# Selections on TensorE for two chunks instead of four, direct placement for three instead of six, softplus written over its exponent in a ring of four tiles

## The chip, the cores and the metric

The kernel runs on one core of a Trainium2 chip. TensorE (PE in the profile, with its weight loads as PEld), VectorE (DVE), ScalarE (ACT), GpSimd (POOL) and the DMA queue that SyncE (SP) issues each work through their own list of instructions in order and meet through semaphores. The metric is the device time of one execution in microseconds; less is better.

## The reference, cut to what matters

Three parts follow one another. The first is a gated linear attention over 4 batches, 8 heads, 768 steps and head size 48: a complex state of 48x48 per head is multiplied at each step by a normed complex gate, the outer product of k and v is added, and q reads the state's real part. The second and third are feed-forward layers over the 3072 tokens of 384 features that come out:

```python
for t in range(S):
    new_re = ar * S_re - ai * S_im
    new_im = ar * S_im + ai * S_re
    S_re, S_im = (new_re + kv, new_im)
    y[:, :, t] = np.einsum('bhd,bhde->bhe', q[:, :, t], S_re)
# x = y as (3072, 384)
h = x @ w_in                                             # 384 -> 2048
g = np.maximum(h, 0.0) + np.log1p(np.exp(-np.abs(h)))    # softplus
x2 = g @ w_out                                           # 2048 -> 384
out = (((x2 @ w1) * (x2 @ w2)) @ w3) @ wo                # 384 -> 1024 -> 384
```

All data are float32 (the weights come as float64 words and are converted on the chip).

## The kernel before, in words

**Stages.** First the product of the last two weights is formed (`early`, tiles wpa, wpe). Phase A then runs over nine blocks of tokens (128, 256, then seven of 384): for each of 16 slices f of the 2048 inner features, `s1` forms h into a PSUM tile s1, ScalarE and VectorE turn it into softplus, and `s2a` adds its product with w_out into three accumulators acc. The first two blocks multiply in plain float32 (native); from block 2 on each operand is split into a high part (xh, gh, ww..h) and a low part (xl, gl, ww..l), and three products replace one. The attention for 24 chunks of 128 tokens (chunk u: 6 chunks per batch) is woven in between and must deliver x for a block before that block can start: chunk 0 for block 0, chunks 1 and 2 for block 1, chunks 3, 4 and 5 for block 2, and so on. Phase B runs the third layer over six blocks of 512 tokens.

**One chunk of attention.** VectorE norms the gates (`norm`, tiles nt, P) and multiplies them up in a scan over pairs of chunks (`scan`, tiles tm, P, E), then forms the scaled q (i = 0) and k (i = 1), real and imaginary, in the tile qkp, of which there is one (`inv`, steps s3 to s5, L641 to L655). Features stand on partitions there in groups of 128, so that heads of 48 straddle them. The tile rs (two of them, taken in turn) wants each head on its own, real part on partitions 0 to 47 and imaginary on 64 to 111. There are two ways: `pick(i)` (L657) selects with small matrices of ones on TensorE into PSUM tiles pk, and ScalarE copies them to rs; `s6` (L673) writes qkp to memory (pd) and reads it back as two transfers into rs. Chunks below `PICK` (L62) go the first way. In `mm(u)` TensorE transposes k (ktp to kT), forms the scores sc, which VectorE masks into am, and `heads` (L714) forms the outputs yp and the state step stp in one group. Chunks below `PLACE` (L63) have the columns of heads 6 and 7 put in their final rows by extra matmuls with the sparse operands ext, and x is read straight from PSUM; later chunks form plain heads, ScalarE copies them to the tile y (one of them) in two pieces, and six small transfers (L762 to L767) move the last two heads into place before x is read.

**Softplus** (L966 to L978). ScalarE writes Abs, Exp and Ln of h into a tile e (a ring of two), VectorE adds max(h, 0) and writes a tile g (a ring of three); from block 2 on ScalarE casts g to gh and VectorE forms gl = g - gh. In blocks 0 and 1 `s2a` reads g itself. The copies of the accumulators at a block's end (xoa) use the ring e as well.

**What sets the order.** Every call is only recorded (`Plan.add`) with a cost of its own and the instructions it must follow. `Plan.flush` orders all of them by a list schedule over 16 rounds of priorities and keeps the order that ends first by its own costs; the instructions are then issued in that order on each engine. Instructions inside `with plan.together()` (L230) form one entry that starts from a base cost. Any edit of what is recorded can therefore move instructions anywhere in the program. All instructions carry the line L207, where the recorded call is made; the tiles tell them apart.

Of the kernel before, what the change touches and what calls it, by code (L numbers as in the profile page):

```python
# [11 lines left out]
F32 = mybir.dt.float32  # L12
# [24 lines left out]
BLOCKS = [(0, 128), (128, 256)] + [(NB * i, NB) for i in range(1, NT // NB)]  # L37
NATIVE = 2
QKB = 1
GB = 3  # L40
HB = 5
AMB = 2
ATT = 5
# [15 lines left out]
CVS = 10  # L59
LEAD = 0  # L60
RATE = 340
PICK = 4  # L62
PLACE = 6  # L63
VW = 6 * 64 + 2 * D
ROUNDS = 16
SEED = 214
# [16 lines left out]
class Plan:  # L83
# [145 lines left out]
    @contextmanager  # L229
    def together(self):  # L230

        self.group = self.push(None, [], set(), 150, 0)
        yield
        self.group = None

# [127 lines left out]
def fused(ctx: ExitStack, tc: tile.TileContext, a_in, qk_in, v_in, wio, w12, w3t, wo2, q, k, v, a_re, a_im, outT):  # L363
# [262 lines left out]
    def inv(u):  # L626
        s = c[u]

        def s1():
            s["n2"] = ap.tile([P, 2, GT], F32, tag="n2", name=f"n2{u}")  # L630
            A.activation(out=s["n2"].rearrange("p c (a l) -> p c a l", l=LN), in_=half(u), func=AF.Square)

        def s2():
            n = s["n2"]
            V.tensor_tensor(out=n[:, 0], in0=n[:, 0], in1=n[:, 1], op=ALU.add)
            if u % CPB == CPB - 1:
                A.copy(pend[:, u // CPB], n[:, 0, GT - LN + J8 - 1 :: J8])
            A.activation(out=n[:, 1], in_=n[:, 0], func=AF.Ln, bias=eps_p)
            A.activation(out=n[:, 1], in_=n[:, 1], func=AF.Exp, scale=-1.0)

        def s3():  # L641
            s["qkp"] = ap.tile([P, 2, G, 2, T], F32, tag="qkp", bufs=QKB, name=f"qkp{u}")
            qkp(u, 0, s["qk"][:, 0])

        def s4():
            n = s["n2"]
            V.tensor_tensor(
                out=in_order(n[:, 0].rearrange("p (g t) -> p g t", t=T)),
                in0=by_group(gt(n[:, 1])),
                in1=in_order(s["qk"][:, 1].rearrange("p (g t) -> p g t", t=T)),  # L650
                op=ALU.mult,
            )

        def s5():
            qkp(u, 1, s["n2"][:, 0])  # L655

        def pick(i):  # L657
            s["rs"] = rs[u % 2]
            for hh in range(2):
                pt = att_ps([P, 4, T], f"pk{u}_{i}_{hh}")  # L660
                with plan.together():
                    for n in range(4):
                        h = 4 * hh + n
                        gs = [g for g in range(G) if (h, g) in sels]
                        for ri in range(2):
                            for g in gs:
                                PE.matmul(
                                    pt[64 * ri : 64 * ri + 64, n], sels[h, g], s["qkp"][:, ri, g, i],
                                    start=g == gs[0], stop=g == gs[-1],
                                )  # L670
                A.copy(s["rs"][:, 4 * hh : 4 * hh + 4, i], pt[0 : 64 + D])

        def s6():  # L673
            s["rs"] = rs[u % 2]
            SP.dma_start(
                pd[u].rearrange("(m p) n -> p m n", p=P), s["qkp"].rearrange("p c g q t -> p (c g) (q t)")
            )
            for ri in range(2):
                SP.dma_start(
                    s["rs"][ri * 64 : ri * 64 + D].rearrange("d h q t -> d h (q t)"),  # L680
                    pd[u][ri * DM : (ri + 1) * DM].rearrange("(h d) n -> d h n", d=D),
                )

        if u < PICK:
            return [s1, s2, s3, lambda: pick(0), s4, s5, lambda: pick(1)]
        return [s1, s2, s3, s4, s5, s6]
# [204 lines left out]
    def early():  # L891
        wo = []
        pieces = []
        for k in range(0, FB, 2):
            r = wp.tile([P, 2 * DM, 2], I32, tag=f"wb{k // 2}", name=f"wor{k}")
            for i in range(2):
                shifted(r[:, i * DM : (i + 1) * DM], wo2[k + i])
            wo.append(r)
        for m0 in range(0, FB, 3):
            n = min(3, FB - m0) * P  # L900
            for k in range(0, FB, 2):
                r = wp.tile([P, 2 * DM, 2], I32, tag=f"wb{4 + len(pieces) % 4}", name=f"w3r{m0}_{k}")[:, 0 : 2 * n]
                for i in range(2):
                    shifted(r[:, i * n : (i + 1) * n], w3t[k + i, :, 2 * m0 * P : 2 * (m0 * P + n)])
                j = len(pieces)
                if m0 == 0:
                    t = wp.tile([P, 2 * DM], F32, tag=f"wa{8 + k // 2}", name=f"wo{k}")
                    convert(t, wo[k // 2], next(ntop) % 2)
                    wo[k // 2] = t
                w = wp.tile([P, 2 * DM], F32, tag=f"wa{12 + j % 3}", name=f"w3_{m0}_{k}")[:, 0 : 2 * n]  # L910
                convert(w, r, next(ntop) % 2)
                pieces.append(w)
                if k == 0:
                    o = [
                        pst(f"acc{i}", 1, [P, NX], f"wpa{m0 + i}") if m0 != 3 else pst("s1", S1B, [P, NX], f"wpa{m0 + i}")
                        for i in range(n // P)
                    ]
                for h in range(2):
                    for i in range(n // P):
                        PE.matmul(  # L920
                            o[i][:, 0:DM], w[:, h * n + i * P : h * n + (i + 1) * P], wo[k // 2][:, h * DM : (h + 1) * DM],
                            start=(k + h == 0), stop=(k + h == FB - 1),
                        )
            for i in range(n // P):
                m = m0 + i
                e = sp.tile([P, NB], F32, tag="e", name=f"wpe{m}")
                A.copy(e, o[i][:, 0:DM])
                SP.dma_start(wpd[m // 2][:, (m % 2) * DM : (m % 2 + 1) * DM], e)

# [16 lines left out]
    def s1(bi, f):  # L946
        _, n = BLOCKS[bi]
        native = bi < NATIVE
        if bi == NATIVE:
            w_split(f)  # L950
        xh, xl = xt[bi]
        pt = pst("s1", S1B, [P, NB], f"s1_{bi}_{f}")
        o = pt[:, 0:n]
        if native:
            prods = [(w32[f], xh)]
        else:
            prods = [(ww[f][0], xh), (ww[f][1], xh), (ww[f][0], xl)]
        i = 0
        for w, xx in prods:
            for k in range(KC):  # L960
                PE.matmul(
                    o, w[:, k * P : (k + 1) * P], xx[:, k, 0:n],
                    start=(i == 0), stop=(i == len(prods) * KC - 1),
                )
                i += 1
        e = sp.tile([P, NB], F32, tag="e", name=f"e_{bi}_{f}")[:, 0:n]  # L966
        A.activation(out=e, in_=o, func=AF.Abs)
        A.activation(out=e, in_=e, func=AF.Exp, scale=-1.0)
        A.activation(out=e, in_=e, func=AF.Ln, bias=1.0)
        g = sp.tile([P, NB], F32, tag="g", bufs=GB, name=f"g_{bi}_{f}")[:, 0:n]  # L970
        V.scalar_tensor_tensor(out=g, in0=o, scalar=0.0, in1=e, op0=ALU.max, op1=ALU.add)
        if native:
            return g, None
        gh = sp.tile([P, NB], F32R, tag="gh", bufs=HB, name=f"gh_{bi}_{f}")[:, 0:n]
        gl = sp.tile([P, NB], F32R, tag="gl", bufs=HB, name=f"gl_{bi}_{f}")[:, 0:n]
        A.copy(gh, g)
        V.tensor_tensor(out=gl, in0=g, in1=gh.bitcast(F32), op=ALU.subtract)
        return gh, gl  # L978
# [75 lines left out]
    for bi in range(nblk):  # L1054
        last = bi == nblk - 1
        t0, n = BLOCKS[bi]
        if not last:
            start = att_pos[0]
            goal = att_end[sum(BLOCKS[bi + 1]) // T - 1] + LEAD
        gq = {}  # L1060
        for f in range(FA):
            if bi == 0:
                if f + 4 < FA:
                    w_load(f + 4)
                if f + 2 < FA:
                    w_piece(f + 2)
            gq[f] = s1(bi, f)
            if f >= 2:
                s2a(bi, f - 2, gq.pop(f - 2))
            if not last:  # L1070
                att_to(start + (goal - start) * (f + 1) // FA)
            else:
                if f >= 6 and f % 2 == 0 and f < 14:
                    wp_load((f - 6) // 2)
                if f >= 7 and f - 7 < FB - 2:
                    w12_conv(f - 7)
        for f in (FA - 2, FA - 1):
            s2a(bi, f, gq.pop(f))
        evac(n, lambda i: x2d[t0 // NB][:, i, t0 % NB : t0 % NB + n], f"a{bi}",
             lambda name: sp.tile([P, NB], F32, tag="e", name=name))  # L1080
    w12_conv(FB - 2)
    w12_conv(FB - 1)

# [344 lines left out]
```

## Time and profile before

| | us |
|---|---|
| median of 3 runs (lowest, highest) | 930.88 (929.62, 932.45) |
| the profiled execution's own time | 930.63 |
| its span, first to last instruction | 928.8 |
| TensorE busy in it | 903.7 |
| VectorE busy in it | 707.8 |
| ScalarE busy in it | 544.4 |

Outside the span lie 930.63 - 928.8 = 1.8 us. The profile records one execution; busy times and waits are of that one. Phase A ends near 630 us. Matmuls overlap: a row says how long one takes from its start to its end, the distance between starts is shorter.

### The profile page before, as it was taken

The numbers are of one execution on the slowest core, as the hardware profiler recorded it, in microseconds if no ns is written. First come the engines' busy times: TensorE is split into PE (matmuls) and PEld (weight loads), VectorE is DVE, ScalarE is ACT, GpSimd is POOL, SyncE is SP. The second block draws the span as 40 slices with busy tenths as digits, with TensorE's granted clock in tenths as the row PEclk, the third lists the DMA queues.
The fourth block names the chain that finished last, engine by engine and source line by source line (L and its number), as shares of the span: only waits on it lengthen the run. The fifth ranks groups of instructions, "written<-read, shape, count | busy, mean of one in ns | idle before, by whom it ended". The sixth has DMA issues, their size and how long they took to land.

```text
span 928.8 us, 16521 instructions
## 1 busy us (share of the span) xinstructions
PE 903.7 (97%) x6081; PEld 815.2 (88%) x6081; DVE 707.8 (76%) x1739; ACT 544.4 (59%) x1111; POOL 10.9 (1%) x31
## 2 busy tenths in 40 slices
PE   3999999999999999999999999999999999999996
PEld 2578988899999999999999999998788887888885
DVE  6999999999999989898988564698888785231221
ACT  6679984678788688678875755872221313131312
POOL 4000000000000000000000000000000000000000
PEclk9999999999999999999999999999999999999999
DMA  9898236265554546437454444248878773000001
GB/s 339 311 320 314 66 109 150 86 148 129 141 150 119 157 115 157 126 98 164 119 153 123 107 119 142 56 137 256 247 257 249 254 232 115 1 35 0 35 1 38
DMA packets 81642, 136.39 MB, mean 147 GB/s; under 512 B 7504, under 2 KB 53136, under 8 KB 81552
## 3 DMA queue, kind: packets, MB, share of 16 engines
q1 hardware_dynamic: 81552, 135.25, 49.4%
q8 instruction: 49, 0.80, 0.4%
q14 instruction: 41, 0.34, 0.1%
HBM read 107.59 MB, written 26.74 MB: 145 GB/s over the span
## 4 chain that ended last, share of the span: by engine, by line
PE 84%; DMA 6%; DVE 5%; ACT 1%; issue 1%; SPq 0%; DVEq 0%; ACTq 0%
PE acc L207 31%; PE s L207 22%; PE pb L207 8%; PE pa L207 8%; PE yp L207 5%; PE sc L207 4%; DMA ckr<-wio 2%; DMA ckr<-w3t 2%; PE stp L207 2%; PE wpa L207 2%; PE pk L207 1%; PE ktp L207 1%; DVE ck L207 1%; DVE tm L207 1%; DVE w L207 1%
## 5 line engine op out<-in xcount | busy, mean ns | idle before, releaser
L207 ACT ACTIVATE e<-e 128x384 f32<-128x384 f32 (+2 forms) x288 | 135.4, 486 | 2.6
L207 DVE TENSOR_TENSOR bg<-pa,bg 128x512 f32<-128x512 f32 x48 | 33.0, 688 | 93.0 <-PE pa L207 82.6
L207 DVE TENSOR_TENSOR tm<-P 128x768 f32<-128x768 f32 (+4 forms) x240 | 101.6, 440 | 1.1
L207 ACT CAST bgg<-bg 128x512 fp32r<-128x512 f32 x48 | 29.8, 621 | 109.7 <-DVE bg L207 109.7
L207 ACT ACTIVATE e<-s 128x384 f32<-128x384 f32 (+2 forms) x144 | 64.9, 453 | 48.6 <-PE s L207 46.3
L207 DVE SCALAR_TENSOR_TENSOR g<-s,e 128x384 f32<-128x384 f32 (+2 forms) x144 | 73.0, 510 | 23.0 <-ACT e L207 21.9
L207 ACT COPY bg<-pb 128x512 f32<-128x512 f32 x48 | 28.2, 588 | 85.3 <-PE pb L207 74.0
L207 DVE TENSOR_TENSOR P<-tm 128x96 f32<-128x96 f32 (+9 forms) x328 | 76.4, 274 | 1.4
L207 DVE TENSOR_TENSOR gl<-g,gh 128x384 fp32r<-128x384 f32 x112 | 61.8, 556 | 9.1 <-ACT gh L207 8.5
L207 ACT CAST gh<-g 128x384 fp32r<-128x384 f32 x112 | 56.5, 507 | 13.1 <-DVE g L207 11.0
L207 PE MATMUL wpa<-wo,w 128*128 128x384 f32 x128 | 44.2, 504 | 14.7 <-DVE w L207 14.7
L207 DVE CUSTOM_DVE_ANT_0 ck<-ckr 128x384 f32<-128x384 f32 x80 | 43.4, 543 | 17.9 <-DMA ckr<-wio 7.8
L207 PE MATMUL sc<-rs 112*128 112x128 f32 x384 | 53.8, 275 | 0.0
L207 PEld LDWEIGHTS wpa<-wo,w 128*128 128x128 f32 x128 | 24.9, 198 | 31.4 <-DVE w L207 14.7
L207 PEld LDWEIGHTS sc<-rs 112*128 112x128 f32 x384 | 51.4, 191 | 0.8 <-issue 0.2
L207 PE MATMUL acc<-bgg,bwp0h 128*128 128x512 f32 x144 | 50.6, 391 | 0.0
L207 PE MATMUL acc<-bgg,bwp2h 128*128 128x512 f32 x144 | 49.0, 391 | 1.2 <-ACT bgg L207 1.2
L207 DVE TENSOR_TENSOR bgg<-bg,bgg 128x512 fp32r<-128x512 f32 x48 | 33.0, 688 | 15.9 <-ACT bgg L207 15.8
L207 DVE TENSOR_REDUCE lims<-ck 128x1 f32<-128x384 f32 x80 | 43.1, 538 | 2.3
L207 DVE TENSOR_TENSOR am<-sc,mask 128x512 f32<-128x512 f32 x48 | 33.1, 689 | 11.6 <-PE sc L207 11.4
L207 PE MATMUL yp<-am,v 128*48 128x128 f32 (+1 forms) x360 | 40.9, 277 | 0.0
L207 PE MATMUL acc<-g,w 128*128 128x128 f32 (+1 forms) x192 | 38.9, 330 | 0.0
(394 smaller groups left out, 2438.3 us busy)
## 6 DMA issues: line engine op xcount, KB each, us to landing
pd<-qkp SPq DMA_DIRECT2D x20, 768.0 KB, 4.3
rs<-pd SPq DMA_DIRECT2D x40, 384.0 KB, 6.0
ckr<-wio SPq DMA_DIRECT2D x32, 384.0 KB, 3.8
wr<-wio SPq DMA_DIRECT2D x32, 383.8 KB, 6.1
a<-a_in SPq DMA_DIRECT2D x24, 384.0 KB, 4.2
qk<-qk_in SPq DMA_DIRECT2D x24, 384.0 KB, 3.3
w12r<-w SPq DMA_DIRECT2D x16, 384.0 KB, 3.2
ckr<-w SPq DMA_DIRECT2D x16, 384.0 KB, 3.7
```

The source lines that it names most:

```text
L207: getattr(engine.unit, op)(*args, **kw)
```

## The change

Three edits, and one in the planner's cost. `PICK` goes from 4 to 2 and `PLACE` from 6 to 3, so that chunks 2 and 3 take the way through memory, and chunks 3, 4 and 5 plain heads with copies and small transfers. `pick` opens both its PSUM tiles at once and puts all 20 matmuls in one group; the base cost of a group rises from 150 to 325. And the ring g is gone: softplus is written over its exponent, e, in a ring of four, which the accumulators' copies and those of the weight product share.

```diff
-GB = 3
+EB = 4
-PICK = 4
-PLACE = 6
+PICK = 2
+PLACE = 3
...
-        self.group = self.push(None, [], set(), 150, 0)
+        self.group = self.push(None, [], set(), 325, 0)
...
         def pick(i):
             s["rs"] = rs[u % 2]
+            pts = [att_ps([P, 4, T], f"pk{u}_{i}_{hh}") for hh in range(2)]
+            with plan.together():
+                for h in range(H):
+                    gs = [g for g in range(G) if (h, g) in sels]
+                    for ri in range(2):
+                        for g in gs:
+                            PE.matmul(
+                                pts[h // 4][64 * ri : 64 * ri + 64, h % 4], sels[h, g], s["qkp"][:, ri, g, i],
+                                start=g == gs[0], stop=g == gs[-1],
+                            )
             for hh in range(2):
-                pt = att_ps([P, 4, T], f"pk{u}_{i}_{hh}")
-                with plan.together():
...
-                A.copy(s["rs"][:, 4 * hh : 4 * hh + 4, i], pt[0 : 64 + D])
+                A.copy(s["rs"][:, 4 * hh : 4 * hh + 4, i], pts[hh][0 : 64 + D])
...
-                e = sp.tile([P, NB], F32, tag="e", name=f"wpe{m}")
+                e = sp.tile([P, NB], F32, tag="e", bufs=EB, name=f"wpe{m}")
...
-        e = sp.tile([P, NB], F32, tag="e", name=f"e_{bi}_{f}")[:, 0:n]
+        e = sp.tile([P, NB], F32, tag="e", bufs=EB, name=f"e_{bi}_{f}")[:, 0:n]
...
-        g = sp.tile([P, NB], F32, tag="g", bufs=GB, name=f"g_{bi}_{f}")[:, 0:n]
+        g = e
         V.scalar_tensor_tensor(out=g, in0=o, scalar=0.0, in1=e, op0=ALU.max, op1=ALU.add)
...
-             lambda name: sp.tile([P, NB], F32, tag="e", name=name))
+             lambda name: sp.tile([P, NB], F32, tag="e", bufs=EB, name=name))
```

How the order moves is shown at three places. In the names the first number is the chunk (sc2, yp2), or the block and the slice f (s1_0_15); the last is a running number. TensorE before, ahead of chunk 2's outputs yp2, which block 1 needs:

```order
L207 MATMUL sc2_1_386<-rs0_144 128x128 x4
L207 MATMUL acc_297<-g_0_13_391,w32_13_373 128x128
L207 MATMUL acc_298<-g_0_12_384,w32_12_365 128x128
L207 MATMUL acc_298<-g_0_13_391,w32_13_373 128x128
L207 MATMUL acc_298<-g_0_14_399,w32_14_381 128x128
L207 MATMUL acc_297<-g_0_14_399,w32_14_381 128x128
L207 MATMUL pk3_0_0_379<-qkp3_369,pick0_142 64x128 x10
L207 MATMUL acc_298<-g_0_15_404,w32_15_388 128x128
L207 MATMUL yp2_393<-am2_0_371,v2_310 64x128
```

TensorE at the same place in the changed order:

```order
L207 MATMUL acc_295<-e_0_14_378,w32_14_363 128x128
L207 MATMUL acc_296<-e_0_14_378,w32_14_363 128x128
L207 MATMUL acc_297<-e_0_14_378,w32_14_363 128x128
L207 MATMUL sc2_0_354<-rs0_144 128x128 x4
L207 MATMUL sc2_1_367<-rs0_144 128x128 x4
L207 MATMUL acc_295<-e_0_15_380,w32_15_370 128x128
L207 MATMUL acc_296<-e_0_15_380,w32_15_370 128x128
L207 MATMUL acc_297<-e_0_15_380,w32_15_370 128x128
L207 MATMUL yp2_373<-am2_0_355,v2_306 64x128
```

Chunk 2's scores stood among block 0's last slices and chunk 3's selections; now nearly all of block 0 stands ahead of them, and only three matmuls between them and yp2.

The queue of SP, where chunk 2 now goes through memory; before, up to chunk 4's transfer:

```order
L207 DMA wr15_372<-wio 128x1535 x2
L207 DMA qk3_346<-qk_in 128x768
L207 DMA v2_310<-v_in 128x480
L207 DMA a6_276<-a_in 128x768
L207 DMA qk4_406<-qk_in 128x768
```

and now:

```order
L207 DMA wr15_357<-wio 128x1535 x2
L207 DMA qk3_334<-qk_in 128x768
L207 DMA v2_306<-v_in 128x480
L207 DMA pd2_67<-qkp2_305 128x6x256
L207 DMA a6_276<-a_in 128x768
L207 DMA rs0_144<-pd2_67 48x8x256 x2
L207 DMA qk4_382<-qk_in 128x768
L207 DMA pd3_68<-qkp3_356 128x6x256
```

The write of chunk 2's products and the two reads behind it follow the last weight loads (wr15), and chunk 3's follow them.

VectorE before, ahead of the last input of block 3 (xl3, low part of x, from chunk 8's y):

```order
L207 TENSOR_TENSOR S8_698<-stp8_696,S7_636 112x384
L207 TENSOR_TENSOR P5_514<-tm_676 128x2x48 x2
L207 TENSOR_TENSOR tm_684<-P5_514 128x192
L207 TENSOR_TENSOR P5_514<-tm_684 128x48 x2
L207 TENSOR_TENSOR tm_687<-P5_514,E_137 128x192 x2
L207 TENSOR_TENSOR P5_514<-tm_687 128x96 x2
L207 TENSOR_TENSOR tm_699<-P5_514 128x288 x2
L207 TENSOR_TENSOR xl3_587<-y8_697,xh3_586 128x3x128
```

and now:

```order
L207 TENSOR_TENSOR S8_646<-stp8_644,S7_590 112x384
L207 TENSOR_TENSOR P5_478<-tm_636 128x96 x2
L207 ISA nt13_614,m2max_132<-nt13_614 128x384
L207 ISA m2max_132 128x1
L207 TENSOR_TENSOR tm_647<-P5_478 128x288 x2
L207 TENSOR_TENSOR P5_478<-tm_647 128x3x48 x2
L207 TENSOR_TENSOR tm_653<-P5_478 128x672
L207 TENSOR_TENSOR P6_577<-nt13_614,P6_577 128x16x24
L207 TENSOR_TENSOR tm_653<-P5_478 128x672
L207 TENSOR_TENSOR xl3_545<-y8_645,xh3_544 128x3x128
```

The scan of chunks 10 and 11 (P5) and the norm of chunk 13 (nt13) stand further along ahead of xl3 than they did.

## Rows read from the trace of the kernel before

**Rows 1.** The page: busy time, share of the span, instructions

```profile
PE 903.7 (97%) x6081; PEld 815.2 (88%) x6081; DVE 707.8 (76%) x1739; ACT 544.4 (59%) x1111; POOL 10.9 (1%) x31
```

**Rows 2.** What waited for whom, longest sum first: us in total, times, longest

```profile
PE wpa L207 <- DVE w L207: 14.7, 1, 14.7
...
PE s L207 <- ACT rs L207: 1.4, 1, 1.4
```

**Rows 3.** Busy time by stretch: busy us (instructions), granted clock, DMA share, GB/s

```profile
core 0: us, PE busy (x) PEld busy (x) DVE busy (x) ACT busy (x) POOL busy (x), PEclk, DMA share, GB/s
20.00:182.70 162.70, 160.99 (x1375) 134.62 (x1373) 155.16 (x408) 122.62 (x268) 0.00 (x0) 1.00 0.59 195
182.70:246.40 63.70, 63.70 (x519) 62.48 (x519) 63.07 (x176) 49.65 (x109) 0.00 (x0) 1.00 0.61 157
246.40:317.10 70.70, 70.41 (x549) 69.01 (x549) 65.51 (x167) 55.33 (x117) 0.00 (x0) 1.00 0.51 134
```

**Rows 4.** Groups of TensorE by shape: busy us, mean ns, idle before

```profile
L207 PE MATMUL pk<-qkp,pick 128*64 128x128 f32 x320 | 20.8, 278 | 0.0
```

**Rows 5.** The chain that ended last, in order of time: start us, us, what

```profile
133.02 3.17 PE yp L207 x45
...
235.75 1.90 PE yp L207 x32
```

**Rows 6.** All engines from 244 us: start us, us, engine, instruction

```profile
245.82 0.55 DVE L207 TENSOR_TENSOR xl<-y,xh 128x384 fp32r<-128x384 f32 x1
...
247.09 0.68 PE L207 MATMUL s<-xh,ww0h 128*128 128x384 f32 x3
...
248.13 0.68 PE L207 MATMUL s<-xl,ww0h 128*128 128x384 f32 x3
```

**Rows 7.** VectorE in order of time from 60 us

```profile
79.42 0.55 DVE L207 CUSTOM_DVE_ANT_0 nt<-nt 128x384 f32<-128x384 f32 x1
...
83.66 0.52 DVE L207 TENSOR_TENSOR P<-tm 128x144 f32<-128x144 f32 x2
84.40 0.85 DVE L207 TENSOR_TENSOR tm<-P 128x672 f32<-128x672 f32 x1
...
94.72 0.55 DVE L207 TENSOR_TENSOR qkp<-P,n 128x384 f32<-128x384 f32 x1
```

**Rows 8.** TensorE in order of time from 10 us

```profile
102.67 1.16 PE L207 MATMUL sc<-rs 112*128 112x128 f32 x8
...
130.26 1.46 PE L207 MATMUL acc<-g,w 128*128 128x256 f32 x6
```

**Rows 9.** Instructions on the tile rs: ns min/median/max, first and last start, forms

```profile
L207 ACT COPY rs<-pk x16: 564/585/592, 55.6 to 123.9; 112x512 f32<-112x512 f32 x16
...
DMA to landing us min/median/max: 4.3/6.0/7.6
```

**Rows 10.** Instructions on the tile qkp: the write to pd

```profile
DMA to landing us min/median/max: 3.7/4.3/5.8
```

**Rows 11.** Busy time by stretch, 80 to 120 us

```profile
80.00:100.00 20.00, 20.00 (x239) 19.25 (x236) 19.49 (x44) 19.20 (x49) 0.00 (x0) 1.00 0.59 215
100.00:120.00 20.00, 20.00 (x254) 18.58 (x255) 17.95 (x59) 18.00 (x41) 0.00 (x0) 1.00 0.17 51
```

**Rows 12.** All engines from 225 us: chunk 7's y, copied, moved and read

```profile
226.61 1.17 ACT L207 COPY y<-yp 48x512 f32<-48x512 f32 x2
...
227.20 4.33 SPq L207 DMA_DIRECT2D y<-y  x6
...
233.91 0.50 ACT L207 CAST xh<-y 128x384 fp32r<-128x384 f32 x1
```

**Rows 13.** Instructions on the tile e

```profile
L207 ACT ACTIVATE e<-e x288: 287/519/551, 73.2 to 620.9; 128x384 f32<-128x384 f32 x112, 128x128 f32<-128x128 f32 x16, 128x256 f32<-128x256 f32 x16
L207 ACT ACTIVATE e<-s x144: 255/490/497, 72.1 to 619.8; 128x384 f32<-128x384 f32 x112, 128x128 f32<-128x128 f32 x16, 128x256 f32<-128x256 f32 x16
L207 DVE SCALAR_TENSOR_TENSOR g<-s,e x144: 281/552/577, 74.0 to 621.8; 128x384 f32<-128x384 f32 x112, 128x128 f32<-128x128 f32 x16, 128x256 f32<-128x256 f32 x16
```

More of the change, by code (lines that the diff above doesn't have):

```diff
@@ L658, in pick @@
             s["rs"] = rs[u % 2]
-            for hh in range(2):
-                pt = att_ps([P, 4, T], f"pk{u}_{i}_{hh}")
-                with plan.together():
[L662 to L670, printed above, removed]
-                A.copy(s["rs"][:, 4 * hh : 4 * hh + 4, i], pt[0 : 64 + D])
+            pts = [att_ps([P, 4, T], f"pk{u}_{i}_{hh}") for hh in range(2)]
[8 more added lines that the diff above has]
+                            )
+            for hh in range(2):
+                A.copy(s["rs"][:, 4 * hh : 4 * hh + 4, i], pts[hh][0 : 64 + D])
         def s6():
```

## The prediction

> **What bounds the kernel now.** I read the busy shares first, then the waits, then the stretches, then single rows. TensorE is busy 903.7 of 928.8 us [rows 1]. The waits say how little of the rest could be saved: 14.7 us before its first matmul, when nothing is converted yet, and one of 1.4 us before block 0 [rows 2], 16.1 of the 25.1 us in which it idles at all. So a microsecond of TensorE work removed in the middle is a microsecond of the program, as long as whoever feeds TensorE keeps up. That is the second thing to see: from 20 to 182.7 us VectorE is busy 155.2 of 162.7 us and from there to 246.4 us 63.1 of 63.7 [rows 3]. Two engines are full side by side, and the change relieves one of them. How close they run is seen at block 3: VectorE ends the last piece of its input at 245.82 + 0.55 = 246.4, TensorE begins with the other pieces at 247.09 and takes this one at 248.13 [rows 6].
>
> **What it removes.** Selections: the four chunks' 160 matmuls, 320 records, come to 20.8 us [rows 4]; half of them go, so -10.4 us. The 278 ns of one record is its length through the array; the sum counts the overlap once, and it is the sum I use. Placement: the outputs of a chunk take 3.17 us with the extra matmuls and 1.90 us without [rows 5]; three chunks, so -3.8 us. Together -14.2 us of TensorE. All of it lies ahead of block 2, where TensorE does not wait but for that 1.4 us. ScalarE loses eight copies of 0.585 us [rows 9], 4.7 us, and some small ones on ext; it gains six of 1.17 / 2 = 0.585 us [rows 12], 3.5 us. It does not hold up anything by that.
>
> **What it adds in transfers.** Chunks 2 and 3 write 768 KB to pd (4.3 us to landing, 5.8 at most [rows 10]) and read it back in two transfers (6.0 us, 7.6 at most [rows 9]). Before, VectorE ended chunk 2's products at 94.72 + 0.55 = 95.3 [rows 7]; in the new order some 2 us less of VectorE work stands ahead, so I take 93.3. With 0.5 us for the issue: 93.8 + 4.3 + 6.0 = 104.1 us, at the worst 107.2. When does TensorE ask? It began these scores at 102.67 [rows 8]; ahead of them the new order has 30 selections fewer, 3.9 us by 0.13 us each [rows 4], and 5.3 us more of block 0, so 104.1. A tie: at most 3 us of standing, and the stretch is free for it, since the transfer engines are at 0.59 up to 100 us and at 0.17 after it [rows 11]. I take 0. The reads are issued by SP, and what is queued behind them (a qk, then chunk 3's own pd) is needed tens of microseconds later. Chunk 3's write may begin once its products are there, and its scores come well inside block 1.
>
> The tile y adds a way of its own for chunks 3 to 5: from the first copy to the cast that reads it 233.91 - 226.61 = 7.3 us pass, about 8 with the cast and a semaphore [rows 12], where x was read straight from PSUM. For chunks 3 and 4 block 1 covers that. For chunk 5 the cover is what stands between its outputs and block 2: twelve products of 256 columns, at 1.46 / 3 = 0.49 us or a little less [rows 8], and three transposes, about 5.6 us. So TensorE stands about 2.4 us there, if it has not stood for VectorE by then; one wait swallows the other, and I don't add them.
>
> **The price at VectorE.** It loses no instruction. TensorE comes to block 3 having done 14.2 us less, but by the order also 24 instructions more of later work (six transposes, the eight scores of chunk 9 and seven products of block 2, 3.7 us by their spacing in the trace): 10.5 us earlier, at 236.6, and it wants the low part of x at 237.6. VectorE must have done more by then, not less. Ahead of that piece the order now has the reduction of chunk 13's norm (0.55), a product with P (0.55 by the same size), two products of 672 elements (0.85 each) and two of 144 (0.26 each) [rows 7]: by start-to-start distance about 2.9 us. So the piece ends at 246.4 + 2.9 = 249.3 if VectorE idles as much as before, and that is 162.7 - 155.2 + 63.7 - 63.1 = 8.2 us from 20 us on [rows 3]. If it never idles, the piece ends at 241.1. TensorE waits, in one place or several up to here, between 241.1 - 237.6 = 3.5 and 11.7 us. Some of VectorE's idle time was spent waiting for TensorE's scores and states, which come sooner now; some for loads in the first 20 us of the stretch, which remains. I take half, a wait of 7.6 us. Later the pressure falls: from 246.4 to 317.1 us VectorE has 5.2 us to spare [rows 3], and it goes on growing.
>
> Where the wait shows: the first place is the order ahead of chunk 2's outputs, where block 0's products no longer lie between the scores and yp2, so that TensorE meets VectorE's two masks and block 0's last softplus directly; then the first products of block 2, then block 3.
>
> **The ring of four.** From block 2 on a tile now lives from Abs to gl: three passes of ScalarE and the add, 0.49 + 2 x 0.52 + 0.55 [rows 13], with a cast and a difference of such a size about 3 us, and waits. A block of 16 slices takes over 60 us, so a slice takes nearly 4 us and four tiles give four times that. In block 0, with some 2 us for a slice, a tile is held until its products are done, and four still give about 8 us for 1.4 us of passes and a queue. I take 0 and give 2 us either way: two tiles of e were tighter than four for the copies at a block's end.
>
> **The sum.** Against the profiled execution, 930.63 us (span 928.8 and 1.8 around it): -14.2 + 7.6 = -6.6, so 924.0. The median of the runs lies 0.25 us above that execution, so 924.3 us.
>
> One rule of the Trainium skill speaks against the 14.2. "Perfetto Trace Analysis", section "Identifying the Most-Contended Engine", says that busy time of matmuls is a poor measure because they are pipelined, and that the busy share of weight loads should be read instead. That is 134.6 of 162.7 us, 83%, up to 182.7 us [rows 3]; by the rule a sixth of that stretch was free, and only about 11.8 of the 14.2 us would come off, 926.4 us in all, as an estimate. The trace does not agree here: in that stretch TensorE's rows follow one another but for 1.7 us, and small fp32 matmuls with short weight loads fill it; I keep 14.2.
>
> **Rivals.** (1) Nothing is lost: VectorE waited mostly for TensorE, its idle time vanishes and the order lets it work ahead. For it: ScalarE, which is at 19.2 of 20 us from 80 to 100 us [rows 11], is relieved too. Against it: even with no idle time 3.5 us stay. 930.9 - 14.2 + 0 to 3.5: about 918.5. (2) No change: VectorE keeps its idle time, TensorE waits 11.7 us, 930.9 - 2.5 = 928.4, and with the 2.4 us for chunk 5's y on top 930.8. For it: two full engines, and a relief of only one; against it: the waits for TensorE among VectorE's. (3) Slower: there is one tile qkp. Chunk 3's products overwrite it, so VectorE must wait until chunk 2's write to pd has landed, and again for chunk 4 behind chunk 3. VectorE's list is in order, and the softplus of blocks 0 and 1 is queued behind. By the order about 6.5 us of other VectorE work lie between the two; a landing of 4.3 us fits, one of 5.8 just so. If SP issues the write late, because it stands behind qk3 and v2 in its queue, and it lands 6 us beyond that cover, both chunks cost 6 us: 924.3 + 12 = 936. It decides from about 7 us after the products' end; what speaks against it is that the transfer engines are nearly free then [rows 11].
>
> **Chances.** My forecast (VectorE gives back a part, 919 to 928) 0.53; nothing lost 0.13; no change 0.19; slower 0.15. A measurement of this kernel tells from no change what exceeds about 0.3%, 2.8 us. Faster takes the first two and a little of the third, 0.68; same 0.17; slower 0.15. The range reaches from 917.5, just short of the whole 14.2 us, up to 932, which holds the no-change case and leaves out most of the slower one; the forecast's own range is 919 to 928.
>
> **What would show it.** In the changed profile: 160 selection records instead of 320, about 10.4 us; the outputs of chunks 3 to 5 at about 1.9 us each; TensorE busy near 889.5 us. New waits of TensorE, 5 to 10 us in sum, all before 250 us and most for VectorE (e, am, gl or xl) rather than for transfers; block 3 beginning at about 243 to 246 us. VectorE's idle time from 20 us to block 3 at about 4 us. Chunk 2's reads landing before 108 us. I am wrong in mechanism if TensorE waits for rs or y longer than 4 us in one place, if waits of that size appear after 320 us, or if VectorE stands before its products for qkp.

## The result, and the profile after

The changed kernel takes 922.14 us (median of 4 runs, 921.03 to 923.35), the kernel before 930.25 us on the same chip (929.24 to 932.45): a ratio of 0.991, 95% interval 0.9885 to 0.9934, 8.1 us faster. 924.3 us were predicted. The time came out near; the experiments show that two parts of the sum were wrong in opposite directions.

The profiled execution took 921.28 us (span 919.5). Its page, busy time of each engine with its share of the span, against [rows 1]:

```profile
PE 890.3 (97%) x5873; PEld 802.6 (87%) x5873; DVE 707.2 (77%) x1739; ACT 539.8 (59%) x1103; POOL 11.3 (1%) x31
```

TensorE is busy 13.4 us less, while the span fell by 9.3: it now stands 29.2 us where it stood 25.1. What it waited for (us in total, times, longest), against [rows 2]:

```profile
PE wpa L207 <- DVE w L207: 13.6, 1, 13.6
PE ktp L207 <- DVE qkp L207: 2.3, 1, 2.3
PE s L207 <- ACT x L207: 1.5, 1, 1.5
PE s L207 <- ACT kT L207: 1.4, 1, 1.4
PE s L207 <- DVE am L207: 1.2, 1, 1.2
PE s L207 <- ACT xh L207: 1.0, 1, 1.0
PE wpa L207 <- DVE wo L207: 0.6, 1, 0.6
PE acc L207 <- DVE e L207: 0.3, 1, 0.3
```

Between the first matmul and block 2 there are now six waits of 0.3 to 2.3 us, 7.3 us in all; before it was 1.7 [rows 3]. The 13.6 us are the start, the wait of 1.0 us for xh comes after 320 us, and the 0.6 us for wo lie in the product of the last two weights. By stretch, up to block 2, to block 3 and to block 4, in the columns of [rows 3]:

```profile
20.00:172.95 152.95, 145.69 (x1164) 119.75 (x1163) 149.93 (x396) 118.67 (x260) 0.00 (x0) 1.00 0.71 229
172.95:242.39 69.44, 69.44 (x553) 68.25 (x551) 68.92 (x193) 53.57 (x114) 0.00 (x0) 0.98 0.56 148
242.39:301.60 59.21, 59.21 (x468) 58.13 (x468) 58.40 (x150) 49.65 (x106) 0.00 (x0) 1.00 0.53 141
```

In the first stretch TensorE stands 7.3 us and VectorE only 3.0; from block 2 to block 4 TensorE does not stand. Selections and outputs, against [rows 4, 5]: the group of TensorE, and three rows of the chain that ended last (a chunk with the extra matmuls, then chunks 3 and 4 without them):

```profile
L207 PE MATMUL pk<-qkp,pick 128*64 128x128 f32 x160 | 9.8, 276 | 0.0
```

```profile
85.41 3.17 PE yp L207 x45
...
129.08 1.90 PE yp L207 x32
...
151.38 1.90 PE yp L207 x32
```

The longest new wait, with chunk 5's y beside it, all engines from 164 us (start us, us, engine, instruction), against [rows 12]:

```profile
164.90 5.45 PE L207 MATMUL acc<-e,w 128*128 128x256 f32 x24
...
165.02 1.19 ACT L207 COPY y<-yp 48x512 f32<-48x512 f32 x2 [0.62 <-PE yp L207]
...
166.07 3.67 SPq L207 DMA_DIRECT2D y<-y  x6
...
171.56 0.52 ACT L207 CAST xh<-y 128x384 fp32r<-128x384 f32 x1
172.04 1.02 DVE L207 TENSOR_TENSOR qkp<-P,n 128x384 f32<-128x384 f32 x2
...
172.65 0.55 PE L207 MATMUL ktp<-ident,qkp 128*128 128x128 f32 x3 [2.30 <-DVE qkp L207]
```

TensorE's last product before it ended at 164.90 + 5.45 = 170.35 us. VectorE, without a gap since 167.8, brings the qkp product only at about 172.6; xh is there at 172.1. The two waits lie over one another. Had qkp been there, TensorE would have done its three short transposes and then stood for xh until about 172.1: the y chain by itself would have kept it standing for more than half of the 2.3 us, and only about 0.8 us (172.95 - 172.1) are VectorE's alone. The wait has a second price. Busy time by 2 us, the granted clock in the column after POOL:

```profile
172.00:174.00 2.00, 1.35 (x9) 1.35 (x10) 2.00 (x6) 0.91 (x3) 0.00 (x0) 0.98 0.71 197
174.00:176.00 2.00, 2.00 (x8) 2.00 (x7) 2.00 (x6) 0.93 (x3) 0.00 (x0) 0.50 1.03 368
176.00:178.00 2.00, 2.00 (x11) 1.97 (x10) 2.00 (x7) 1.44 (x5) 0.00 (x0) 0.66 0.38 122
178.00:180.00 2.00, 2.00 (x14) 1.97 (x13) 2.00 (x8) 2.00 (x5) 0.00 (x0) 1.00 1.07 205
```

After the stand the granted clock falls from 1.00 to 0.50 (2.4 to 1.2 GHz): by these rows an estimated 2 x (0.02 + 0.50 + 0.34) = 1.7 us of TensorE's work is lost, and it is counted as busy time.

### The profile page after: what moved, and what is told of

The parts are those of the page before. It is cut to its first block, busy times and chain, and to the rows that moved or that the text cites. A ratio compares the mean times of both kernels' runs of the same rounds, so it can differ in the third digit from the quotient of the medians.

```text
span 919.5 us, 16096 instructions
## 1 busy us (share of the span) xinstructions
PE 890.3 (97%) x5873; PEld 802.6 (87%) x5873; DVE 707.2 (77%) x1739; ACT 539.8 (59%) x1103; POOL 11.3 (1%) x31
## 4 chain that ended last, share of the span: by engine, by line
PE 87%; DVE 5%; ACT 3%; DMA 2%; issue 1%; SPq 1%; DVEq 0%; ACTq 0%
PE acc L207 32%; PE s L207 22%; PE pa L207 11%; PE pb L207 11%; PE yp L207 4%; PE sc L207 4%; PE stp L207 2%; DVE tm L207 2%; DMA w3r<-w3t 1%; PE ktp L207 1%; DVE P L207 1%; DVE w L207 1%; SPq L207 1%; DVE qkp L207 0%; ACT wtop_ws L207 0%
## 5 line engine op out<-in xcount | busy, mean ns | idle before, releaser
L207 DVE SCALAR_TENSOR_TENSOR e<-s,e 128x384 f32<-128x384 f32 (+2 forms) x144 | 72.0, 506 | 18.0 <-ACT e L207 17.5
L207 DVE TENSOR_TENSOR gl<-e,gh 128x384 fp32r<-128x384 f32 x112 | 61.4, 552 | 7.2 <-ACT gh L207 6.4
L207 ACT CAST gh<-e 128x384 fp32r<-128x384 f32 x112 | 56.6, 508 | 15.2 <-DVE e L207 15.1
L207 PE MATMUL wpa<-wo,w 128*128 128x384 f32 x128 | 45.0, 506 | 14.1 <-DVE w L207 13.6
L207 PE MATMUL s<-x,w 128*128 128x128 f32 (+1 forms) x192 | 37.4, 330 | 4.1 <-ACT x L207 1.5
L207 PE MATMUL yp<-am,v 128*48 128x128 f32 (+1 forms) x372 | 37.8, 274 | 0.1
```

Source lines behind the costliest of these rows:

```text
L207: getattr(engine.unit, op)(*args, **kw)
```

## The experiments

Theory A is the prediction's: the two numbers (PICK, PLACE) take 14.2 us off TensorE, and VectorE, full beside it up to block 3, takes back about half. Its first rival is that ring, grouping and order carry the gain.

**The change in two halves.** e1_sel_place is the kernel before with

```
-PICK = 4
-PLACE = 6
+PICK = 2
+PLACE = 3
```

> The kernel before with only the two numbers changed (PICK 2, PLACE 3); it keeps the separate ring for g and the selections in two groups a tile. Theory A (TensorE work removed, 14.2 us, and VectorE, which is full beside it up to block 3, takes back about half): 922 to 925 us, TensorE busy near 889.5 us, TensorE waits before 250 us of 5 to 10 us for VectorE. Rival B (the ring of four and the new grouping, and the order that they give, carry a good part of the gain): 926 us or more.

e2_ring_group is the changed kernel with these two lines put back, so that only the ring and the one-group form (with its base cost of 325) remain.

> The changed kernel with the two numbers put back (PICK 4, PLACE 6): only the ring of four and the one-group form of the selections remain. Theory A: 929 to 932 us, within 0.3% of before, TensorE busy 903 to 904 us. Rival B: 926 us or less, since part of the gain would stay.

Measured: e1 925.82 us (ratio 0.995, 0.9931 to 0.9968), e2 926.38 us (0.9953, 0.9936 to 0.9971). Both miss what theory A expected, and both lie just short of rival B's bound: the numbers alone give 4.6 us, not 6.6, and the part that was priced at nothing gives 4.1. Together that is 8.7 us, near the 8.1 of the whole change. The pages, e1's and then e2's:

```profile
PE 892.4 (97%) x5873; PEld 804.6 (87%) x5873; DVE 706.8 (76%) x1739; ACT 542.2 (59%) x1103; POOL 11.5 (1%) x31
```

```profile
PE 900.8 (98%) x6081; PEld 815.2 (88%) x6081; DVE 707.7 (77%) x1739; ACT 545.1 (59%) x1111; POOL 10.4 (1%) x31
```

In e1 TensorE is busy 11.3 us less and stands 31.9 us (span 924.3) instead of 25.1. In e2 it does the same matmuls as before in 2.9 us less and stands 21.6 us (span 922.4). From e2 to the changed kernel, then, its idle time grows by 29.2 - 21.6 = 7.6 us. (e2's profiled run was the fastest of its six, 2.2 us below their median, so this difference holds for these two executions only.) e1's longest wait after the first matmul, and the clock behind it:

```profile
PE s L207 <- DVE g L207: 3.7, 1, 3.7
```

```profile
94.00:96.00 2.00, 0.99 (x7) 0.99 (x8) 2.00 (x5) 2.00 (x4) 0.00 (x0) 0.91 0.89 334
96.00:98.00 2.00, 1.40 (x7) 1.10 (x6) 2.00 (x4) 2.00 (x5) 0.00 (x0) 0.50 0.56 196
98.00:100.00 2.00, 1.64 (x7) 1.65 (x8) 2.00 (x6) 1.31 (x4) 0.00 (x0) 0.50 0.43 116
100.00:102.00 2.00, 2.00 (x12) 2.00 (x11) 1.24 (x4) 1.96 (x7) 0.00 (x0) 0.50 1.10 201
```

**Each number alone**, on the kernel before. e3_sel_only:

```
-PICK = 4
+PICK = 2
```

> The kernel before with PICK 2 alone: 80 selection matmuls fewer (10.4 us), and two chunks more through pd. Theory A: the 10.4 us come off TensorE's busy time (893 us) and VectorE takes back 3 to 6 us, so 923.5 to 927.5 us. Rival C (the trip through pd and the reads of rs hold TensorE up): waits of TensorE for rs or of VectorE before its products for qkp of over 4 us in one place, and 928 us or more.

e4_place_only:

```
-PLACE = 6
+PLACE = 3
```

> The kernel before with PLACE 3 alone: three chunks without the extra matmuls (3.8 us), and y for them. Theory A: the low part of x for block 3 is ready 1.7 us before TensorE takes it in the kernel before, so of 3.8 us about 1.7 to 3.8 come off: 926.5 to 928.5 us, TensorE busy near 900 us. Rival D (chunk 5's copy, DMA and cast of y stand open, 2.4 us): 929.5 to 931.5 us, with a wait of TensorE for y, xh or ktp of 2 us or more.

Measured: e3 924.53 us (0.9936, 0.9919 to 0.9952), within what theory A said. TensorE is busy 894.3 us, 9.4 less, and stands 28.0 us, 2.9 more, mostly for g, am and qkp, not for rs; VectorE waits 0.2 us in all for a write to pd. Rival C falls, and with it the prediction's slower rival (one tile qkp). e4 930.04 us (0.9991, 0.998 to 1.0003): 0.4 us, no difference that can be told. Its busy time falls by 3.0 us and its idle time grows by 3.1. The time is rival D's, and the largest new wait is at chunk 5's y, as rival D said, if shorter than its 2 us; it is about half of the 3.1. So what the two numbers give comes from the selections (e3 alone gave 5.9 us, more than e1 with both); no run shows a gain from the placement. All engines of e4 from 168 us:

```profile
168.62 0.58 ACT L207 COPY y<-yp 48x512 f32<-48x512 f32 x1 [0.58 <-DVE tm L207]
...
170.88 3.67 SPq L207 DMA_DIRECT2D y<-y  x6
...
177.02 0.50 ACT L207 CAST xh<-y 128x384 fp32r<-128x384 f32 x1
...
177.57 0.79 PE L207 MATMUL s<-xh,ww0h 128*128 128x384 f32 x3 [1.68 <-ACT xh L207]
```

From the first copy to the first product 9.0 us pass, and 1.68 of them stand open.

**The ring alone, and another order.** e5_ring_only, on the kernel before (all three tiles e with bufs=EB):

```
-GB = 3
+EB = 4
-        g = sp.tile([P, NB], F32, tag="g", bufs=GB, name=f"g_{bi}_{f}")[:, 0:n]
+        g = e
```

> The kernel before with the ring alone: e in four tiles, the softplus's sum written over e, no tiles g; selections in two groups a tile as before. The ring of four and the one-group form together had given 926.4 us (4.1 us off) without removing any matmul. If the ring does that (copies of a block's end and the first softplus of the next no longer stand in line for two tiles of e): 926 to 927.5 us, first matmul near 13.8 us instead of 14.7, waits of TensorE after 320 us below 1.5 us. If the one-group form does it: 929.5 to 931.5 us.

e6_before_seed and e7_after_seed are the kernel before and the changed one with

```
-SEED = 214
+SEED = 1
```

> The kernel before, the planner's noise drawn from another seed (1 instead of 214): the same instructions in another order. If the 4.1 us of ring and group form are within what any other order gives: 926 us or less, or 934 us or more. If an order is worth little by itself: 929 to 932 us.

> The changed kernel with the same other seed (1). If the gain of 8 us belongs to the work and the ring: 920.5 to 924 us, and 7 to 10 us below the kernel before with that seed. If a good part of it is the luck of one order: 925 us or more.

e12_ring_seed is e5 with that seed.

> The ring alone on the kernel before, with the planner's other seed (1). If the ring itself is worth its 3.5 us: 924 to 925.5 us, 3 to 4 us below the kernel before with that seed (928.4). If it only gave another order: 926.5 to 930 us.

Measured: e5 926.89 us (0.9966, 0.9953 to 0.9979), so the ring does most of e2's 4.1 us, and the rest, 0.5 us, can't be told from nothing. Of the two signs one came (first matmul at 13.6 us) and one did not: after 320 us TensorE waits 2.2 us, 1.6 of it in a new wait for gh. e6 928.39 us (0.9986, 0.9976 to 0.9996), between its two cases: another order alone moves the kernel before by 1.3 us by the ratio, 2.0 between the medians. e7 922.76 us (0.9925, 0.9912 to 0.9938), e12 926.51 us (0.9952, 0.9933 to 0.997): e12 lies at the edge of its second case, and e7 is within its first range but only 5.6 us below e6, where 7 to 10 were expected. By the medians the ring is worth 3.5 us with seed 214 and the numbers on top of ring and grouping 4.2; with seed 1 the ring is worth 1.9 and the rest of the change 3.8. By the ratios the ring is worth 3.2 us with either seed (e6 less e12 with seed 1), the numbers 4.0, and the rest of the change with seed 1 2.5. Each ratio is uncertain by 1 to 2 us, so both parts show in both orders, and that the ring's part depends on the order is not shown.

One place where the ring works can be seen. ScalarE's copies of the last block of the first stage, before:

```profile
626.50 1.08 ACT L207 COPY xoa<-acc 128x384 f32<-128x384 f32 x2
...
631.33 0.48 ACT L207 COPY xoa<-acc 128x384 f32<-128x384 f32 x1 [2.04 <-DMA x2d<-xoa]
```

and in e5:

```profile
621.96 0.86 ACT L207 COPY xoa<-acc 128x384 f32<-128x384 f32 x2 [0.59 <-PE acc L207]
623.71 0.48 ACT L207 COPY xoa<-acc 128x384 f32<-128x384 f32 x1 [0.88 <-PE acc L207]
```

Three copies go through tiles e. With two of them the third comes 4.8 us after the first two, behind the store of one, and ScalarE's queue stands 2.0 us; with four it comes 1.75 us after. TensorE's waits for ScalarE's bgg behind it are 1.2 us before, 0.6 in e5 and none in e2 and in the changed kernel. That is part of the ring's gain. In all, e5 stands 2.4 us less than the kernel before (22.7 us) and is busy 2.2 us less with the same matmuls; why it is less busy, and how much of the idle time goes with the order, was not isolated.

**VectorE relieved.** e8_after_gpsimd, in the changed kernel:

```
-        split(ww[f][0], ww[f][1], w32[f])
+        A.copy(ww[f][0], w32[f])
+        GP.tensor_tensor(out=ww[f][1], in0=w32[f], in1=ww[f][0].bitcast(F32), op=ALU.subtract)
```

> The changed kernel with the sixteen differences for the weights' low parts (0.95 us each, 15.2 us, from 102.9 to 226 us) moved from VectorE to GpSimd, which stands idle there. Theory A (VectorE is what holds TensorE up before block 3): the wait of 2.3 us for qkp and the fall of the clock behind it go (another 1.7 us), the small waits before 100 us stay: 916.5 to 919.5 us. Rival E (the waits are set by ScalarE or transfers, or a slower GpSimd holds the splits up): 921 us or more.

Measured: 945.81 us (1.0167, 1.0154 to 1.0181), 24 us slower than the changed kernel. It was no relief, and the traces show a reason that rival E did not name. VectorE and then GpSimd in e8, from 128 us:

```profile
128.15 0.41 DVE L207 SCALAR_TENSOR_TENSOR e<-s,e 128x256 f32<-128x256 f32 x1
128.48 2.56 DVE L207 TENSOR_TENSOR qkp<-P,n 128x384 f32<-128x384 f32 x2
130.97 2.17 DVE L207 TENSOR_TENSOR P<-nt,P 128x384 f32<-128x384 f32 x1
133.17 0.56 DVE L207 SCALAR_TENSOR_TENSOR P<-P,nt 128x384 f32<-128x384 f32 x1
```

```profile
128.34 1.82 POOL L207 TENSOR_TENSOR ww1l<-w,ww0h 128x768 fp32r<-128x768 f32 x1 [17.88 <-PE acc L207]
130.49 2.23 POOL L207 TENSOR_TENSOR ww2l<-w,ww2h 128x768 fp32r<-128x768 f32 x1 [0.33 <-PE acc L207]
```

The first of the two products takes 2.09 us (the second 0.54, as ever), and the product behind them 2.17 instead of 0.55: both end 0.4 us after the subtraction on GpSimd that began just before them. VectorE lost 15 us of work and is busy 721.0 us instead of 707.2. The Trainium skill says it ("SBUF — State Buffer", section "Who interferes with whom"): a VectorE instruction with two inputs in SBUF contends with a GpSimd instruction that reads SBUF. The trace agrees, with these numbers. As a test of theory A the run counts only the other way round: 13.8 us more of VectorE's time cost 24 us.

e9_after_relief takes the work away instead, in the changed kernel, and e10_ring_group_relief does so in e2:

```
     def w_split(f):
-        ww[f] = w_tiles(f, f"ww{f}")
-        split(ww[f][0], ww[f][1], w32[f])
+        if f == 0:
+            ww[f] = w_tiles(f, f"ww{f}")
+            split(ww[f][0], ww[f][1], w32[f])
+            return
+        ...
+        ww[f] = whp[f // 2][:, f % 2], ww[0][1]
+        A.copy(ww[f][0], w32[f])
```

> The changed kernel with 15 of VectorE's 16 differences for the low parts of the first stage's weights left out: the products with low parts of slices 1 to 15 read slice 0's low part, so the result is not the reference's, and TensorE and ScalarE do the same work. VectorE loses 15 x 0.95 = 14.2 us before block 3 and nothing takes their place. Theory A (what the two numbers save at TensorE, VectorE partly takes back): TensorE's waits for am, qkp and e (3.8 us) and the fall of the clock (1.7 us) go: 916.5 to 919.5 us. Rival E (those waits are set by ScalarE, transfers or the order): 920.5 us or more.

> The same differences left out of the kernel with ring and group form alone (PICK 4, PLACE 6; 926.4 us; the result is not the reference's there either). TensorE waits 1.0 us in it after its first matmul, so theory A: 924.5 to 926.5 us, and the two numbers, worth 4.2 us without relief, are worth 7 to 10 us with it (against the run with PICK 2 and PLACE 3). Rival E: both kernels gain alike, by 0 to 2 us, and the numbers stay at about 4 us.

Measured: e9 917.12 us (0.9853, 0.9826 to 0.988), e10 926.25 us (0.9951, 0.9933 to 0.997). The same relief gives the changed kernel 5.0 us and e2 0.1. The two numbers, worth 4.2 us, are worth 9.1 us where VectorE is relieved of differences of 14.2 us in all; its busy time falls by 10.5 us in e9 and 9.4 in e10. The times are theory A's, not rival E's. The waits of TensorE, e9's and then e10's:

```profile
PE wpa L207 <- DVE w L207: 13.9, 1, 13.9
PE acc L207 <- DVE e L207: 1.5, 1, 1.5
PE s L207 <- ACT xh L207: 1.0, 1, 1.0
PE s L207 <- DVE e L207: 0.8, 2, 0.5
PE sc L207 <- DVE am L207: 0.2, 1, 0.2
```

```profile
PE wpa L207 <- DVE w L207: 12.8, 1, 12.8
PE s L207 <- ACT xh L207: 1.0, 1, 1.0
PE s L207 <- DVE am L207: 0.3, 1, 0.3
...
```

TensorE is busy 889.1 us in e9 and 902.1 in e10, 13.0 us apart, and stands 25.2 and 21.3 us; 13.0 - 3.9 = 9.1. The edit also frees the products from waiting for the low parts' tiles, and both kernels were planned anew. In e9 TensorE comes to block 2 like this:

```profile
166.43 0.82 PE L207 MATMUL ktp<-ident,qkp 128*128 128x128 f32 x6
167.08 2.76 PE L207 MATMUL acc<-e,w 128*128 128x256 f32 x12
169.49 0.88 PE L207 MATMUL s<-xh,ww0h 128*128 128x384 f32 x3
```

With qkp there earlier, the transposes stand 2.5 us ahead of the first product with xh, so the wait for y's chain is covered as well. ScalarE does the same work in e9, and the two waits for it are gone too. So the 4.9 us between the two reliefs are what VectorE's work costs through the order it forces, not VectorE's time alone, and one order of each kernel was measured.

**The placement on top.** e11_after_place6 is the changed kernel with

```
-PLACE = 3
+PLACE = 6
```

> The changed kernel with PLACE put back to 6: selections, ring and group form remain, the extra matmuls of chunks 3 to 5 come back (3.8 us) and the y of these chunks goes. Alone PLACE 3 gave 0.4 us, beside PICK 2 it cost 1.3 us. If that holds here: 920.5 to 922 us. If the placement pays its 3.8 us or half of it: 924 to 926 us.

Measured: 922.86 us (0.9914, 0.9894 to 0.9935), between the two cases, 0.7 us above the changed kernel and not to be told from it. TensorE is busy 893.9 us, 3.6 more, and stands 27.0, 2.2 less. No variant beat the changed kernel without leaving work out.

## Why the prediction was right, and where it was wrong

- **The removal, -14.2 us.** Selections 20.8 to 9.8 us, three chunks' outputs 3.17 to 1.90: as worked out. In busy time -13.4 from before to after, of which 2.9 came with ring and grouping alone; between kernels with the same ring -13.0 (e10 to e9) and -10.5 (e2 to after), where 1.7 us of the difference is the clock and some 2 stay unexplained. These figures lie on both sides of the 11.8 us that the busy share of the weight loads gave, so they do not decide between the two readings (the time by that share should have read 926.7 us; 0.25 us of the median were left out). But the placement's -3.8 us, though they left TensorE, never came off the time: 0.4 us alone, 1.3 the other way beside PICK 2, 0.7 beside PICK 2 and the ring, none of them clear of noise.
- **The price at VectorE, +7.6 us.** Right that TensorE runs into the engines beside it; that the size came out to the tenth is luck. It was half of the way between two bounds, 3.5 and 11.7 us. Against e2, which differs by the numbers alone, TensorE's idle time grows by 7.6 us in the two profiled executions, nearly all of it before block 2; with 10.5 us less of busy time that leaves 2.9 us there, and 4.2 between the medians. Block 3, from which the term was worked out, begins at 242.39 (243 to 246 said) and without a wait: the low part of x, which VectorE starts at 242.24, is used only at 243.97. Of the waits, 3.8 us are for VectorE (qkp, the masks, e), with chunk 5's y under the longest, and 2.9 us are two waits of 1.4 us (up to 80.45) and 1.5 us (up to 114.50) for ScalarE, which is busy 6.95 of 7 us from 74 to 81 and all of 106 to 115. For ScalarE I had said that the change makes it hold up nothing, and that was wrong.
- **Not in the sum: the clock.** A stand of TensorE was priced at its length. The one of 2.3 us cost 1.7 us more, the one of 3.65 us in e1 up to 2 x (0.09 + 3 x 0.50) = 3.2, both estimates from their rows. With it the numbers give -14.2 + 7.6 + 1.7 = -4.9; -4.2 was measured on top of the ring (ratios uncertain by 1.6 and 2.3 us) and -4.6 without it, where the sum had -6.6.
- **The ring, 0 us with 2 either way.** This step failed in size: -3.5 us (2.0 to 4.4), -1.9 to -3.2 in another order. A part of the reason was among the words ("two tiles of e were tighter than four for the copies at a block's end") and I gave it no value; the rest stays open. So it is in part luck that 924.3 came near 922.1: the numbers paid some 2 us less than said, and the ring with the grouping some 4 us more.
- **Transfers, 0 us.** Right for rs: chunk 2's write was issued at 90.71 us and its reads at 95.24, and its scores began at 105.78 without a wait. Chunk 5's y fell together with the wait for qkp, as said; it would have held TensorE for more than half of that wait in any case, and alone (e4) 1.68 us of it stood open.
- **The rivals.** "Nothing lost" would have been 918.5, and even e9 leaves 2.5 us of waits for VectorE. "No change" fits the placement by itself (e4), not the whole. The slower one (qkp's single tile) did not come about: 0.2 us in e3, none after.

## What to carry to other kernels

Where two engines are full side by side, work removed from one need not pay: here 14.2 us paid 4.2, and 9.1 once the second engine was relieved. Ask of each piece what stands behind it: selections paid, and the placement, which put a chain of transfers in place of its matmuls, did not. Price a new stand of TensorE with the slower clock that may follow it, and give a pool that grows from two tiles to four a value of its own; copies that wait for a store are one sign of it (0.6 to 1.2 us of 3.5 here). Where order is planned anew with each edit, run a second seed: here an order alone was worth 1.3 to 2.0 us, up to a quarter of the whole gain.

## What the hardware showed unexpectedly

The granted clock fell to 0.50 to 0.54 behind stands of TensorE of 2.30 us (changed kernel), 3.65 us (e1), and 2.45, 3.01, 3.04 and 5.16 us (e8); behind stands of 1.40 and 1.51 us (changed kernel), 1.68 us (e4) and also 2.41 us (e8) no stretch of 2 us was below 0.97. In e7 it fell to 0.53 behind one of 1.83 us, so the length of the stand alone does not tell. A subtraction of 128x768 elements on GpSimd, 1.8 us or more, held the two-input instruction that VectorE began behind it until the subtraction was done (a product of 128x12 elements took 1.78 us instead of 0.17).
